# A recurrent-memory transformer layer on one core: rider queries' transposes, a store of extra rows and the tail's loads are moved in the queues

## The chip, the cores and the metric

The kernel runs on one core of one Trainium2 chip. The metric is the device time of one execution in microseconds (us). A core has five engines with an instruction stream each: TensorE (PE), VectorE (DVE), ScalarE (ACT), GpSimd (POOL) and SyncE (SP). Here SP and POOL mostly issue DMA transfers, which 16 DMA engines carry out.

## The reference

One layer on a sequence of 2048 tokens of width 640: attention with a recurrent memory, then a gated feed-forward network (FFN) of width 1728. Weights and inputs are bf16.

```python
mem = mem0                                   # 8 memory rows
for s in range(64):                          # segments of 32 tokens
    h = concatenate([mem, LN(x)[32*s : 32*s+32]])          # 40 rows
    q, k, v = h @ Wq, h @ Wk, h @ Wv         # 32 heads of 128
    p = softmax(mask(q @ k.T / sqrt(128)))   # memory rows see all; tokens: memory and earlier ones
    o = (p @ v) @ Wo
    mem = o[:8]; out[s] = o[8:]
h = x + out
y = h + ((relu(LN(h) @ Wg) * (LN(h) @ Wu)) @ Wd)
```

The memory of segment s + 1 is an output of segment s, so the 64 segments form a chain. Only the eight memory rows are in the chain: the projections of the tokens are not.

## The kernel before, in words

**Passes.** The loop over s makes one *pass* for each segment. TensorE projects 32 columns at a time: the 8 memory rows of segment s and 24 *riders*, rows of tokens that a later segment needs. As 24 riders a pass are fewer than the 32 tokens that a segment takes, a fourth kind of work, the *extra units*, projects 32 more tokens in three passes of four (`extra_units`: keys in phase s % 4 = 2, queries in phase 3, values in phase 0). In phase 1 the same place holds `woe_pass`, the output projection of the memory rows of four segments (the *extra rows*), summed by `woe_sum` in the tile `at` and stored by `woe_store`. `filler` puts these units between the steps of the softmax, so that TensorE has work while other engines run.

A pass has this order on TensorE: K projection into banks BQ; Q projection into P0 and P1; `pick_mem` (L450), which takes the memory rows' queries out of the token tiles; V projection; `scores` (L569); memory probabilities times V (L606) among the filler; their transposes (L621); the output projection `wo_pass` (L641, 128 short matmuls); `pv_x` (L679). The result of `wo_pass` makes the memory rows of the next pass (`to_act`).

**Transposes by DMA.** Projections come out with tokens on the partitions, and are wanted the other way round. ACT and DVE copy them to `tok` tiles (`to_tok`), tiles 0 and 1 for K, 2 and 3 for Q, and also 2 and 3 for the extra units. SP's queue then issues `dma_t`, a crossbar transpose by DMA (L360): K's into `KS`, the attention output's into `oT`, the rider queries' into `QS` (`trans_q`), and in phases 2 and 3 those of the extra units into a tile `Kr` or again into `QS`. From `QS`, `evac_q` copies the riders' queries into the ring `Qr` on ACT. The V riders go by POOL's DMAs (`v_riders`). In the kernel before, `trans_q` comes right behind the Q projection in program order, and `evac_q` behind `exp_x`.

**Order and waits.** `_Graph` records each operation with the names it reads and writes, and each engine runs its own in program order. `solve` sets a wait wherever an operation reads what another engine wrote, writes what it reads, or overwrites it. An operation put on an engine's queue holds back all that follow it there. The lists `late` and `late_q` hold operations that are recorded in the next pass, behind the transposes of K and of `oT`, and behind the Q copies. `align` puts spare weight loads into TensorE's stream so that marked places in `wo_pass` (`MARKS`) lie at fixed places of blocks of 256 instructions.

**Tail.** In the last passes the FFN weights are loaded over the projection weights. `load_gate_up` loads `xn2T`, `Wg`, `Wu` and `Wgu`; `gate_up(0, j)` are the first FFN products, mixed with the last segments' output projections and extra rows; `ln2_load` loads rows of x and attention for the second layer norm; `h_rows` and `Wd` are loaded for the down projection.

Of the kernel before, what the change touches and what calls it, by code (L numbers as in the profile page):

```python
# [206 lines left out]
def build_kernel(nc, A_x, A_mem0, A_Wq, A_Wk, A_Wv, A_Wo, A_seg_len, B_W_gate, B_W_up, B_W_down, out):  # L207
    _, S, D = A_x.shape
    M = A_mem0.shape[1]
    _, H, Dh = A_Wq.shape  # L210
    SEG = int(A_seg_len)
    F = B_W_gate.shape[1]
    assert (S, D, M, H, Dh, SEG, F) == (2048, 640, 8, 32, 128, 32, 1728)
    NSEG = S // SEG
    DC = D // 128
    HD = H * Dh
    FC = (F + 127) // 128
# [82 lines left out]
    def bank_bf(b):  # L300
        return ps[:, b * 512:(b + 1) * 512].bitcast(BF16)
# [14 lines left out]
    def B(n):  # L316
        return ("B", n)
# [38 lines left out]
    def dma(dst, src, r=(), w=(), eng="sp"):  # L356
        add(eng, lambda e: e.dma_start(dst, src), r=r, w=w, dma=True)  # L357
# [94 lines left out]
            return ins  # L452
        add("pe", f, r=[("tok", 2), ("tok", 3), ("ident",)], w=[B(bk)])

    def trans_q():
        dma_t(QS[:].rearrange("p h t -> p (h t)").rearrange("p (k r) -> p k r", r=128), tokp[1][:, :],
              [("tok", 2), ("tok", 3)], [("QS",)])

    def copy_op(eng, dst, src, r, w):
        if eng == "act":  # L460
# [21 lines left out]
    def evac_q(src, skey, t0, n, lo, eng):  # L482
        for q, o, m, lo in pieces(t0, n, lo):
            copy_op(eng, Qr[:, :, q, M + o:M + o + m], src[:, :, lo:lo + m], [skey], [("Qr", q)])
# [93 lines left out]
    def exp_mem():  # L578
        add("act", lambda a: a.activation(ap(om, 0, [[8, 2], [16, 8], [1, 8]]), s_view(0, M), ACTF.Exp,
                                          scale=SCALE), r=[B(P0), B(P1)], w=[("om",)])  # L580
        for i in range(2):
            add("dve", lambda v, i=i: v.tensor_tensor(ap(Pbd, 256 * i, [[32, 8], [16, 2], [1, 16]]),
                                                      ap(om, 0, [[16, 8], [0, 2], [1, 16]]),
                                                      ap(mbd, 32 * i, [[0, 8], [16, 2], [1, 16]]), ALU.min),
                r=[("om",), ("mbd",)], w=[("Pbd", i)])

    def exp_x():
        add("act", lambda a: a.activation(ap(Px, 0, [[32, 2], [64, 8], [1, 32]]), s_view(M, M + SEG),  # L588
# [28 lines left out]
    def trans_om(tile):  # L617
        for a, b in enumerate((T0, P3)):
            def f(pe, a=a, b=b):
                for c in range(0, 128, tile):  # L620
                    i = pe.matmul(bank_bf(b)[c:c + tile, 0:128], om[:, a, c:c + tile], ident[:, :], is_transpose=True)  # L621
                return i
            add("pe", f, r=[("om",), ("ident",)], w=[B(b)])
        for a, b in enumerate((T0, P3)):
            copy_op("dve", ap(oT, 8 * SEG * a, [[2 * SEG, 4], [16 * SEG, 2], [SEG, 2], [1, M]]),
                    bank_bf(b)[:, 0:128].rearrange("p (k g e q) -> p k g e q", k=4, g=2, e=2), [B(b)], [("oT", "mn"[a])])

    def head_of(n):

# [34 lines left out]
    def store_attn(src, skey, s):  # L664

        dma(bass.AP(attn_d, SEG * s * D, [[160, 4], [D, SEG], [1, 160]]), src[:].rearrange("p c j -> p (c j)"), r=[skey],
            w=[("attn", s)], eng="pool")
# [60 lines left out]
    def load_attn(dst, i, r, key):  # L728
        dma(dst[:, :], attn_d[128 * i:128 * i + 128, :, :].rearrange("t g f -> t (g f)"), r=attn_keys(i) + r, w=[key])

    def ln2_load(i):
        u = i % 4
        dma(xt2[u][:, :], x_ap[128 * i:128 * i + 128, :], r=[("Wdone", 1), ("Wu", DC - 1)], w=[("xt2", u)])
        load_attn(at2[u], i, [("Wdone", 1), ("Wu", DC - 1)], ("at2", u))

    def ln2_front(i):
        par, u = (i // 4) % 2, i % 4
# [94 lines left out]

    def load_gate_up(after):
        free = [("Wdone", 0)] + after
        dma(xn2T[0][:, :, :], xn2_d[:, :, :], r=[("xn2_d", u) for u in range(4)] + free,
            w=[("xn2", 0, u) for u in range(4)], eng="pool")
        for n, (t, src) in enumerate(((Wg, B_W_gate), (Wu, B_W_up))):
            for c in range(DC):
                dma(t[:, c, :], src[128 * c:128 * c + 128, 0:FM], r=free, w=[(("Wg", "Wu")[n], c)], eng="pool")
            dma(Wgu[:, :, n * FR:(n + 1) * FR], src.rearrange("(c p) f -> p c f", p=128)[:, :, FM:F],  # L840
                r=free, w=[("Wgu", n)], eng="pool")

    PARTS = tuple((c,) for c in range(DC))
    WPARTS = (range(0, 3), range(3, 6), range(6, 9), range(9, 13), range(13, 16))
# [38 lines left out]
        add("dve", lambda v: v.tensor_tensor(bass.AP(at, 0, [[D, 64], [1, 320]]), tmp, bank(bk)[0:64, 0:320], ALU.add),  # L883
            r=[B(bk), ("at",)], w=[("at",)])

    def woe_store(b):
        for dg in range(2):
            dma(bass.AP(attn_d, 128 * b * D + 320 * dg, [[SEG * D, 4], [D, M], [1, 320]]),
                bass.AP(at, 32 * dg * D, [[D, 32], [1, 320]]), r=[("at",)] + [("attn", 4 * b + j) for j in range(4)],
                w=[("attne", b, dg)], eng="pool")  # L890

    late, late_q = [], []
    for s in range(NSEG):
# [20 lines left out]
        if s > 0:  # L914
            a, ks, kn = pass_act(s)
            t0, nr = rider_tokens(s)
            project(a, ks, 1, (0, 1), BQ, (0, 1), spare=16)
            ks = ks + kn
            project(a, ks, 1, (0, 1), BQ, (2, 3, 4), spare=24)
            to_tok(BQ[0], 0, "act")  # L920
            to_tok(BQ[1], 1, "dve")
            if last:
                break
            dma_t(KS[:].rearrange("p h t -> p (h t)").rearrange("p (k r) -> p k r", r=128), tokp[0][:, :],
                  [("tok", 0), ("tok", 1)], [("KS",)])
            trans_ox()
            for f in late:
                f()
            late = []
            project(a, ks, 0, (0, 1), (P0, P1), spare=40)  # L930
            to_tok(P0, 2, "act")
            to_tok(P1, 3, "dve")
            for f in late_q:
                f()
            late_q = []
            if nr and s < NSEG - 2:
                trans_q()
            loads()
            project(a, ks, 2, (0, 1), (P2, P3), (0, 1), spare=16)
            if s == NSEG - 2:  # L940
                trans8(tok[2], ("tok", 2), tok[3], ("tok", 3), T0)
                copy_op("dve", Qr[:, :, q, 0:M], slots(T0, 0, M), [B(T0)], [("Qm", q)])
                evac_q(slots(T0, 0, SEG), B(T0), t0, nr, M, "act")
            else:
                pick_mem(T0)
                copy_op("dve", Qr[:, :, q, 0:M], bank(T0)[:, 0:256].rearrange("p (h t) -> p h t", t=M), [B(T0)], [("Qm", q)])
            if nr:
                evac_k(KS, ("KS",), t0, nr, M, "dve")
            project(a, ks, 2, (0, 1), (P2, P3), (2, 3, 4), spare=24)
            to_v(P3, Vp, 1, ("Vp", 3), "dve")  # L950
            to_v(P2, Vp, 0, ("Vp", 0), "act", 0, 2)
            scores(s)
            exp_mem()
            to_v(P2, Vp, 0, ("Vp", 1), "act", 2, 4)
            exp_x()
            if nr:
                v_riders(t0, nr)
                if s < NSEG - 2:
                    evac_q(QS, ("QS",), t0, nr, M, "act")
        units, evac, nfin = extra_units(s)  # L960
        woe = s % 4 == 1 and s >= 5

# [9 lines left out]
            copy_op("dve", oTn[:, :, :], oT[:, :, 0:M], [("oT", "m"), ("oT", "n")], [("oTn",)])  # L972
        elif s > 0:
            copy_oTe(s - 1)
        if s == NSEG - 2:
            load_gate_up([("oTe", (s - 1) % 4)])
        norm_om()
        filler(2)
        filler(3)
        trans_om(128 if s % 4 < 2 else 32)  # L980
        mask_x()
        n = n_rows(nb) if s % 4 == 2 and ln else 128 if e2b is not None else 0
        if n:
# [4 lines left out]
        if woe:  # L988
            copy_op("dve", oTe[:, :, 0:M], oTn[:, :, :], [("oTn",)], [("oTe", 0)])
            woe_sum(BQ[0])  # L990
            woe_store(s // 4 - 1)
        wo_pass(T1, MARKS[s % 4] if s > 0 else None)
        to_act(s + 1, B(T1), bank(T1)[:, 0:160])
        if s >= 1:
            wo_rows(T1, wtok[s % 2], ("wtok", s % 2), "act")
            store_attn(wtok[s % 2], ("wtok", s % 2), s - 1)
        pv_x(s, P0)
        if n:
            dma_t(chunks_of(at[:, :])[:, :, 0:n], xt[0:n, :], [("xt",)], [("at",)])
# [76 lines left out]
    def rows(bk, p, s):  # L1076
        wo_rows(bk, wtok[p], ("wtok", p), "act")
        store_attn(wtok[p], ("wtok", p), s)
# [14 lines left out]
    pv_x(s, P0)  # L1093
    copy_op("act", oTe[:, :, M * ((s - 1) % 4):M * ((s - 1) % 4) + M], QS[:, :, 0:M], [("QS",)], [("oTe", (s - 1) % 4)])
    norm_x(P0)
    wo_pass(BQ[1], None, QS, [[("QS",)]] * 2, (0,))
    trans_pe(oT, [("oT", "m"), ("oT", "n"), ("oT", "x")])
    wo_pass(BQ[1], None, QS, [[("QS",)]] * 2, (1,))
    rows(BQ[1], 0, s - 1)
    copy_oTe(s)  # L1100
    gate_up(0, 0)
    for i in range(4, 8):
        ln2_load(i)
    dma(h_rows[0][:, :, :], h_d[:, :].rearrange("(u p) d -> p u d", p=128), r=[("h_d", u) for u in range(4)] +
        [("Wdone", 1), ("Wu", DC - 1)], w=[("h", 0, u) for u in range(4)], eng="pool")
    dma(Wd[:, 0:FC - 1, :], B_W_down[0:FM, :].rearrange("(j p) d -> p j d", p=128),
        r=[("Wdone", 1)], w=[("Wd", 0)], eng="pool")
    dma(Wd[FR:128, FC - 1, :], B_W_down[FM:F, :], r=[("Wdone", 1)], w=[("Wd", 1)], eng="pool")
    wo_pass(P0)
    rows(P0, 1, s)  # L1110
    gate_up(0, 1)
    woe_pass(P3, range(16))
    woe_sum(P3)
    woe_store(NSEG // 4 - 1)
    gate_up(0, 2)
    gate_up(0, 3)
    for par in range(2):
# [83 lines left out]
```

## Time and profile before

| | value |
|---|---|
| time, median of 3 runs | 1107.48 us (1104.06 to 1113.91) |
| span of the profiled run | 1109.9 us |
| TensorE clock, mean | 0.992 of full speed |
| PE busy | 1054.9 us |
| DVE, ACT, POOL busy | 608.7, 365.7, 290.5 us |
| matmuls of the K, Q and V projections (L419, L397; act_r) | 4277 x 384 ns, 3603 x 379 ns, overlapping |
| SP's transposes into QS, KS, oT | 76, 62 and 62; 3.2, 3.2 and 2.8 us to landing |
| POOL's V rider copies | 376 |
| share of the 16 DMA engines' span: SP's queue, POOL's queue | 41.2%, 9.3% |

The page lists, per engine, how long it was busy, and per group of instructions what ended the idle time before them. "Idle before <- X" names the last semaphore that came; "issue" names a wait that no semaphore in the profile explains. A DMA's time runs from the start of its issue to its landing. PEld is the weight load that goes with each matmul.

### The profile page before, as it was taken

The numbers are of one execution on the slowest core, as the hardware profiler recorded it, in microseconds if no ns is written. First come the engines' busy times: TensorE is split into PE (matmuls) and PEld (weight loads), VectorE is DVE, ScalarE is ACT, GpSimd is POOL, SyncE is SP. The second block draws the span as 40 slices with busy tenths as digits, with TensorE's granted clock in tenths as the row PEclk, the third lists the DMA queues.
The fourth block names the chain that finished last, engine by engine and source line by source line (L and its number), as shares of the span: only waits on it lengthen the run. The fifth ranks groups of instructions, "written<-read, shape, count | busy, mean of one in ns | idle before, by whom it ended". The sixth has DMA issues, their size and how long they took to land.

```text
span 1109.9 us, 56106 instructions
## 1 busy us (share of the span) xinstructions
PE 1054.9 (95%) x28040; PEld 510.8 (46%) x23478; DVE 608.7 (55%) x1673; ACT 365.7 (33%) x794; POOL 290.5 (26%) x583
## 2 busy tenths in 40 slices
PE   4679999999999999999999999999999998999998
PEld 3344544444545454545454445444444454444443
DVE  3245656565556565666666666565656553553532
ACT  1214333433343433333334333334333332231211
POOL 1013333333333332323232323232324151000000
PEclk9979999999999999999999999999999999999999
DMA  9936464646463636465756665554545557132100
GB/s 362 377 84 111 88 109 89 105 90 107 81 110 80 115 79 110 83 123 100 119 103 116 104 114 107 93 92 97 94 92 96 93 159 240 39 80 75 27 18 25
DMA packets 287788, 121.65 MB, mean 110 GB/s; under 512 B 263968, under 2 KB 277184, under 8 KB 287552
## 3 DMA queue, kind: packets, MB, share of 16 engines
q1 hardware_dynamic: 267824, 93.92, 41.2%
q0 software_dynamic: 19312, 23.89, 9.3%
q8 instruction: 202, 3.31, 1.2%
q14 instruction: 34, 0.28, 0.1%
q10 hardware_dynamic: 416, 0.26, 0.1%
HBM read 36.79 MB, written 7.21 MB: 40 GB/s over the span
## 4 chain that ended last, share of the span: by engine, by line
PE 86%; DMA 8%; SPq 3%; issue 1%; POOL 1%; DVE 1%; ACT 1%; DVEq 0%; ACTq 0%
PE ps L419 24%; PE ps L397 23%; PE ps L641 13%; PE ps L1030 10%; PE ps L655 3%; PE ps L679 3%; PE ps L569 3%; PE ps L1062 3%; DMA Wo<-in_A_Wo_dram 3%; SPq L357 3%; PE ps L606 2%; DMA QS<-tok 2%; DMA KS<-tok 2%; PE ps L450 2%; PE ps L621 1%
## 5 line engine op out<-in xcount | busy, mean ns | idle before, releaser
L419 PE MATMUL ps<-W,act_r 128*32 128x512 bf16 x4277 | 399.1, 384 | 8.8 <-DMA W<-in_A_Wv_dram 2.5
L397 PE MATMUL ps<-W,act_r 128*32 128x512 bf16 x3603 | 356.9, 379 | 0.3
L357 POOL DMA_DIRECT2D Vr<-Vp x376 | 187.6, 506 | 449.7 <-ACT Px L588 396.9
L419 PEld LDWEIGHTS ps<-W,act_r 128*32 128x32 bf16 x4277 | 121.5, 97 | 262.2 <-issue 170.2
L461 ACT ACTIVATE tok<-ps 128x512 bf16<-128x512 f32 x191 | 110.3, 594 | 237.2 <-PE ps L397 204.7
L641 PE MATMUL ps<-Wo,oT 128*32 128x160 bf16 x8192 | 161.8, 236 | 14.6 <-DMA Wo<-in_A_Wo_dram 8.0
L641 PEld LDWEIGHTS ps<-Wo,oT 128*32 128x32 bf16 x8192 | 147.0, 98 | 36.6 <-issue 16.7
L463 DVE CAST tok<-ps 128x512 bf16<-128x512 f32 x131 | 90.5, 691 | 131.5 <-PE ps L397 109.9
L461 ACT ACTIVATE Qr<-QS 128x512 bf16<-128x512 bf16 (+3 forms) x107 | 70.1, 682 | 61.0 <-DMA QS<-tok 60.5
L419 PE MATMUL ps<-W,act_e 128*32 128x512 bf16 x900 | 89.6, 381 | 0.0
L397 PE MATMUL ps<-W,act_e 128*32 128x512 bf16 x900 | 89.1, 379 | 0.0
L552 DVE STREAM_TRANSPOSE TBf<-ps 128x64 f32<-128x64 f32 (+1 forms) x128 | 33.5, 262 | 93.9 <-PE ps L641 93.8
L694 DVE TENSOR_TENSOR ox<-ps,rx 128x512 bf16<-128x512 f32 x128 | 82.4, 685 | 2.2
L461 ACT ACTIVATE Vp<-ps 128x256 bf16<-128x256 f32 (+1 forms) x126 | 48.5, 385 | 104.7 <-PE ps L397 102.2
L357 POOL DMA_DIRECT2D attn_d<-wtok x64 | 46.6, 728 | 126.8 <-ACT wtok L461 126.6
L1045 DVE TENSOR_TENSOR hT<-g,ps 128x512 bf16<-128x512 bf16 (+1 forms) x56 | 38.5, 688 | 53.7 <-PE ps L1030 49.8
L1030 PE MATMUL ps<-xn2T,Wu 128*128 128x512 bf16 x260 | 64.6, 379 | 0.0
L1030 PE MATMUL ps<-xn2T,Wg 128*128 128x512 bf16 x246 | 61.6, 379 | 1.1 <-issue 0.3
L1043 ACT ACTIVATE g<-ps 128x512 bf16<-128x512 f32 (+1 forms) x56 | 32.4, 592 | 89.4 <-PE ps L1030 89.4
L397 PE MATMUL ps<-Wd,hT 128*128 128x320 bf16 x224 | 61.0, 299 | 0.0
L1062 PE MATMUL ps<-Wd,hT 128*128 128x320 bf16 x224 | 61.0, 299 | 0.0
L463 DVE CAST Vp<-ps 128x512 bf16<-128x512 f32 x64 | 44.2, 691 | 30.4 <-PE ps L397 24.5
(114 smaller groups left out, 1145.8 us busy)
## 6 DMA issues: line engine op xcount, KB each, us to landing
Vr<-Vp POOLq DMA_DIRECT2D x124, 48.8 KB, 2.3
W<-in_A_Wk_dram SPq DMA_DIRECT2D x2, 2560.0 KB, 13.2
W<-in_A_Wq_dram SPq DMA_DIRECT2D x2, 2560.0 KB, 29.3
W<-in_A_Wv_dram SPq DMA_DIRECT2D x2, 2560.0 KB, 28.1
Wo<-in_A_Wo_dram SPq DMA_DIRECT2D x2, 2560.0 KB, 28.5
xt<-in_A_x_dram SPq DMA_DIRECT2D x30, 160.0 KB, 3.6
Vr<-Vp POOLq DMA_DIRECT2D x128, 32.5 KB, 1.9
attn_d<-wtok POOLq DMA_DIRECT2D x64, 40.0 KB, 2.9
```

The source lines that it names most:

```text
L357: add(eng, lambda e: e.dma_start(dst, src), r=r, w=w, dma=True)
L397: return pe.add_instruction(mybir.InstMatmult(name=nc.get_next_instruction_name(), engine=mybir.EngineType.PE, ins=[pe.lower_ap(rhs), pe.l ...
L419: ins = pe.matmul(*a, start=(c == 0), stop=(c == DC - 1), skip_group_check=True)
L461: add("act", lambda a: a.activation(dst, src, ACTF.Copy), r=r, w=w)
L463: add("dve", lambda v: v.tensor_copy(dst, src), r=r, w=w)
L552: add("dve", lambda v, lo=lo, hi=hi: v.transpose(TBf[:, lo:hi, :].rearrange("p c t -> p (c t)"), src[:, 32 * lo:32 * hi]), r=[wkey], w=[(" ...
L569: i = pe.matmul(bank((P0, P1)[g % 2])[p:p + (M if a else 32), 40 * k:40 * k + 40], lh, Qr[:, h, q, :], start=True, stop=True, skip_group_c ...
L641: i = pe.matmul(bank(bk)[32 * gg:32 * gg + 32, 0:160], src[:, hb, :], w[:, gg], start=(hb == ORDER[0]), stop=(hb == ORDER[31]), skip_group ...
L694: add("dve", lambda v, kh=kh: v.tensor_tensor(ox[:, :, kh, :], src[:, :, kh, 0:128], ap(rx, kh, [[2, 4], [0, 128]]), ALU.mult), r=[B(b0 + ...
L1030: ins = pe.matmul(bank(bk), w[:, c, lo:lo + 128], xn2T[par][:, c, :], start=(c == 0), stop=(c == DC - 1))
L1045: add("dve", lambda v: v.tensor_tensor(hT[par][lo:128, j, :], g1[gi][lo:128, :], bank(bu)[lo:128, :], ALU.mult), r=[B(bu), ("g1", gi)], w= ...
L1062: i = pe.matmul(*a, start=(j == 0), stop=(j == FC - 1), skip_group_check=True)
```

## The change

It does four things to the order of work; nothing computed is changed.

1. `trans_q` of the riders moves from behind the Q projection to behind `v_riders`, and waits for a new name, `("qgo", 1)`, which the second operation on the memory probabilities (`Pbd`, L582) writes. The purpose is that this transpose runs after the probabilities of the memory rows, not beside the transposes of K and `oT`. Its `evac_q` on ACT moves behind `wo_rows` and `store_attn`.
2. `woe_store` is put into `late` with a read of `KS`: it goes when K's transpose in the next pass has landed.
3. `load_gate_up` is issued by SP instead of POOL, after the copies of `trans_om` (`("go", 1)`), and the small `Wgu` loads come last.
4. In the tail, `gate_up(0, 0)` comes before the last two segments' output projections; the loads of x, attention rows, `h_rows` and `Wd` wait for the last `woe_sum` (`("at",)`).

```diff
-    def trans_q():
+    def trans_q(after=()):
         dma_t(QS[:].rearrange("p h t -> p (h t)").rearrange("p (k r) -> p k r", r=128), tokp[1][:, :],
-              [("tok", 2), ("tok", 3)], [("QS",)])
+              [("tok", 2), ("tok", 3)] + list(after), [("QS",)])
...
-                r=[("om",), ("mbd",)], w=[("Pbd", i)])
+                r=[("om",), ("mbd",)], w=[("Pbd", i), ("qgo", i)])
...
-        dma(xt2[u][:, :], x_ap[128 * i:128 * i + 128, :], r=[("Wdone", 1), ("Wu", DC - 1)], w=[("xt2", u)])
-        load_attn(at2[u], i, [("Wdone", 1), ("Wu", DC - 1)], ("at2", u))
+        dma(xt2[u][:, :], x_ap[128 * i:128 * i + 128, :], r=[("Wdone", 1), ("at",)], w=[("xt2", u)])
+        load_attn(at2[u], i, [("Wdone", 1), ("at",)], ("at2", u))
...
-        dma(xn2T[0][:, :, :], xn2_d[:, :, :], r=[("xn2_d", u) for u in range(4)] + free,
-            w=[("xn2", 0, u) for u in range(4)], eng="pool")
-        for n, (t, src) in enumerate(((Wg, B_W_gate), (Wu, B_W_up))):
+        dma(xn2T[0][:, :, :], xn2_d[:, :, :], r=[("xn2_d", u) for u in range(4)] + free, w=[("xn2", 0, u) for u in range(4)])
+        both = (("Wg", Wg, B_W_gate), ("Wu", Wu, B_W_up))
+        for k, t, src in both:
             for c in range(DC):
-                dma(t[:, c, :], src[128 * c:128 * c + 128, 0:FM], r=free, w=[(("Wg", "Wu")[n], c)], eng="pool")
+                dma(t[:, c, :], src[128 * c:128 * c + 128, 0:FM], r=free, w=[(k, c)])
+        for n, (k, t, src) in enumerate(both):
             dma(Wgu[:, :, n * FR:(n + 1) * FR], src.rearrange("(c p) f -> p c f", p=128)[:, :, FM:F],
-                r=free, w=[("Wgu", n)], eng="pool")
+                r=free, w=[("Wgu", n)])
...
-    def woe_store(b):
+    def woe_store(b, after=()):
...
-            if nr and s < NSEG - 2:
-                trans_q()
             loads()
...
             if nr:
                 v_riders(t0, nr)
                 if s < NSEG - 2:
-                    evac_q(QS, ("QS",), t0, nr, M, "act")
+                    trans_q([("qgo", 1)])
...
-        if s == NSEG - 2:
-            load_gate_up([("oTe", (s - 1) % 4)])
         norm_om()
...
         trans_om(128 if s % 4 < 2 else 32)
+        if s == NSEG - 2:
+            load_gate_up([("oTe", (s - 1) % 4), ("go", 1)])
...
-            woe_store(s // 4 - 1)
+            late.append(lambda b=s // 4 - 1: woe_store(b, [("KS",)]))
...
             store_attn(wtok[s % 2], ("wtok", s % 2), s - 1)
+            if nr and s < NSEG - 2:
+                evac_q(QS, ("QS",), t0, nr, M, "act")
...
+    gate_up(0, 0)
     wo_pass(BQ[1], None, QS, [[("QS",)]] * 2, (0,))
     trans_pe(oT, [("oT", "m"), ("oT", "n"), ("oT", "x")])
     wo_pass(BQ[1], None, QS, [[("QS",)]] * 2, (1,))
     rows(BQ[1], 0, s - 1)
     copy_oTe(s)
-    gate_up(0, 0)
+    gate_up(0, 1)
+    wo_pass(P0)
+    rows(P0, 1, s)
+    woe_pass(P3, range(16))
+    woe_sum(P3)
+    woe_store(NSEG // 4 - 1)
     for i in range(4, 8):
         ln2_load(i)
     dma(h_rows[0][:, :, :], h_d[:, :].rearrange("(u p) d -> p u d", p=128), r=[("h_d", u) for u in range(4)] +
-        [("Wdone", 1), ("Wu", DC - 1)], w=[("h", 0, u) for u in range(4)], eng="pool")
+        [("Wdone", 1), ("at",)], w=[("h", 0, u) for u in range(4)], eng="pool")
     dma(Wd[:, 0:FC - 1, :], B_W_down[0:FM, :].rearrange("(j p) d -> p j d", p=128),
-        r=[("Wdone", 1)], w=[("Wd", 0)], eng="pool")
-    dma(Wd[FR:128, FC - 1, :], B_W_down[FM:F, :], r=[("Wdone", 1)], w=[("Wd", 1)], eng="pool")
-    wo_pass(P0)
-    rows(P0, 1, s)
-    gate_up(0, 1)
-    woe_pass(P3, range(16))
-    woe_sum(P3)
-    woe_store(NSEG // 4 - 1)
+        r=[("Wdone", 1), ("at",)], w=[("Wd", 0)], eng="pool")
+    dma(Wd[FR:128, FC - 1, :], B_W_down[FM:F, :], r=[("Wdone", 1), ("at",)], w=[("Wd", 1)], eng="pool")
```

More of the change, by code (lines that the diff above doesn't have):

```diff
@@ L625, in trans_om @@
             copy_op("dve", ap(oT, 8 * SEG * a, [[2 * SEG, 4], [16 * SEG, 2], [SEG, 2], [1, M]]),
-                    bank_bf(b)[:, 0:128].rearrange("p (k g e q) -> p k g e q", k=4, g=2, e=2), [B(b)], [("oT", "mn"[a])])
+                    bank_bf(b)[:, 0:128].rearrange("p (k g e q) -> p k g e q", k=4, g=2, e=2), [B(b)], [("oT", "mn"[a]), ("go", a)])
     def head_of(n):
@@ L884, in woe_sum @@
             r=[B(bk), ("at",)], w=[("at",)])
-    def woe_store(b):
+    def woe_store(b, after=()):
         for dg in range(2):
             dma(bass.AP(attn_d, 128 * b * D + 320 * dg, [[SEG * D, 4], [D, M], [1, 320]]),
-                bass.AP(at, 32 * dg * D, [[D, 32], [1, 320]]), r=[("at",)] + [("attn", 4 * b + j) for j in range(4)],
+                bass.AP(at, 32 * dg * D, [[D, 32], [1, 320]]), r=[("at",)] + [("attn", 4 * b + j) for j in range(4)] + list(after),
                 w=[("attne", b, dg)], eng="pool")
```

## The prediction

> **What bounds the kernel now.** I read the page first (busy shares, chain, queues), then the list of waits for PE, then PE's rows in order of time, cut into passes at L679 (the last block of a pass), and last the DMA packets beside the rows.
>
> ```profile
> span 1109.9 us, 56106 instructions
> PE 1054.9 (95%) x28040; PEld 510.8 (46%) x23478; DVE 608.7 (55%) x1673; ACT 365.7 (33%) x794; POOL 290.5 (26%) x583
> q8 instruction: 202, 3.31, 1.2%
> L461 ACT ACTIVATE Qr<-QS 128x512 bf16<-128x512 bf16 (+3 forms) x107 | 70.1, 682 | 61.0 <-DMA QS<-tok 60.5
> QS<-tok SPq DMA_TRANSPOSE x76, 3.2
> ```
>
> PE is busy 95% at a clock of 0.99: no other engine bounds the span, and only PE's holes can be won. The third line is PE's own instruction stream, fetched by DMA: 3.31 MB in 202 packets, 16.4 KB each. The last two say that ACT sits idle 60.5 us before copies out of QS, a transpose that takes 3.2 us from issue to landing.
>
> Between 92 and 895 us there are 60 whole passes, four phases (s % 4) of 15. Their means and minima are 13.53 and 13.23, 13.81 and 13.30, 13.60 and 13.20, 13.52 and 13.10 us, so 15 x (0.30 + 0.51 + 0.40 + 0.42) = 24.5 us lie above the best passes. By block, above the block's own minimum: output projection (L641, least 2.32 us) 10.5 us, of it 6.7 in phase 1; first projection (least 5.30) 6.1 us, of it 4.6 in phase 2; the projection before the scores 2.7; P.V (L679) 2.7. Pass 29, which began at 443.6, shows the cause, in the timeline:
>
> ```profile
> 450.20 1.27 SPq L360 DMA_TRANSPOSE QS<-tok  x1
> 451.73 0.49 DVE L582 TENSOR_TENSOR Pbd<-om,mbd 128x256 bf16<-128x256 bf16 x2 [0.29 <-ACT om L579]
> 452.56 3.95 POOL L357 DMA_DIRECT2D Vr<-Vp  x8 [7.43 <-ACT Px L588]
> 454.10 1.07 PE L641 MATMUL ps<-Wo,oT 128*32 128x160 bf16 x52
> 455.62 0.94 ACT L461 ACTIVATE Qr<-QS 128x256 bf16<-128x256 bf16 x2 [3.16 <-DMA QS<-tok]
> 455.84 1.50 PE L641 MATMUL ps<-Wo,oT 128*32 128x160 bf16 x76 [0.67 <-issue]
> 457.81 1.25 POOL L357 DMA_DIRECT2D attn_d<-at  x2 [1.30 <-DVE TBf L552]
> ```
>
> PE stops after 52 of 128 matmuls, with "issue" as the reason: nothing it waits for is late except its own instructions. The fetch packet for that place ran at 452.95 to 454.42, behind the QS transpose, whose packets filled all 16 DMA engines from 451.5 to 453.4. In passes that do not stop the same packet begins near 8.4 us after the pass's start; here at 9.3. The tail has the same hole:
>
> ```profile
> 919.25 0.94 PE L641 MATMUL ps<-Wo,QS 128*32 128x160 bf16 x43
> 922.55 0.58 PE L641 MATMUL ps<-Wo,QS 128*32 128x160 bf16 x21 [2.37 <-issue]
> 923.29 1.03 PE L1030 MATMUL ps<-xn2T,Wg 128*128 128x512 bf16 x4 [0.16 <-DMA Wu<-in_B_W_up_dram]
> ```
>
> Here 2.37 us go by while the FFN weights fill the DMA engines.
>
> **The Trainium skill.** "Runtime: NRT & Kernel Launch", section Instruction fetch mechanics: an engine's instructions come in blocks of 16 KiB, 256 instructions, over its own DMA queue, and crossing a block is mostly hidden. The trace agrees on the size; that it is hidden it contradicts where transposes are in the way (0.67 us above). "DMA: Bandwidth & Descriptors", section Queues, rings and completion order: each DMA engine takes packets from its queues in turn, so a fetch, a transpose and a GpSimd copy share it. The trace agrees: QS transposes that meet a fetch land in 4.6 to 5.5 us, the others in 3.1 to 3.2. "Advanced Engine Details and Errata", section Sequencer and Instruction Queues: a queued engine instruction waits for its semaphores before it goes; here ACT's copy above waited 3.16 us with the L882 copy of the extra rows behind it.
>
> **The change, part by part.**
>
> (1) *QS transpose later.* It now waits for the second L582 op, which ends 8.58 us into a pass, not 5.8 to 6.9. The second fetch (8.4 to 9.4) is then ahead of it. The transpose spends some 1.25 us on issue (its SPq row), so its packets lie at about 9.9 to 11.7, and the third fetch comes at 11.9 or later in undisturbed passes. I take 8 of the 10.5 us of the output projection as won, and 3.7 of the 4.6 us of phase 2, whose holes lie 20 matmuls into the pass, at a block's edge: they are the third fetch of phase 1, late because the second was. The rest stays for chance collisions. Sum -11.7.
>
> (2) *ACT's Qr copies after `wtok`.* The same 107 copies; they now run at 0.5 to 1.3 us of the next pass, ahead of that pass's first tok copy at 2.38 us, so they hide there. ACT no longer holds the extra units' copies (BQ) behind QS. Passes 36 and 47 lost 0.84 and 1.0 us in P.V's tail that way: -1.8.
>
> (3) *New wait.* The extra units of phases 2 and 3 write tok 2 and 3 on ACT, and now must wait for the QS transpose that reads them. Issue 8.60 + 3.2 = 11.8; two copies, 1.08 us, end at 12.9; PE needs the banks at 13.1 to 13.2, so landings up to 3.37 us are free. With the landings of KS (54 readable, median 3.2, three over 3.6) the overrun is 1.8 us over 30 passes; with those of today's QS (19 of 47 over 3.6) 15 us. KS has a fetch ahead of it, as QS will: I take 4.
>
> (4) *Second QS transpose of phase 3.* It overwrites QS, so it waits for the copies of (2): 0.47 + 0.84 = 1.31 us into phase 0, where it used to start before the pass began. Behind it: PE's pick of the memory rows (L450) needs tok 2 and 3, written at 4.54, and these wait for the landing. 1.31 + 3.05 (the least) = 4.36 costs nothing; with the 15 late landings of today (3.05 to 5.47) the mean overrun is 0.54, 8 us in all. A fetch begins at 2.05 or later in that phase, while the transpose is still being issued; such cases land in 3.5 to 3.9, 0.3 to 0.65 us too late: I take 0.4 x 15 = +6. Pass 48 shows the price: PE waited 0.5 us for a QS landing 4.97 us in.
>
> (5) *Extra rows' store after KS.* 15 x 2 DMAs, 0.61 us of POOL each, nothing behind them until the V copies at 8.9 us, so the move is free. In pass 18 two row stores lay under KS, which landed in 4.91 us, not 3.2, and PE lost 1.25 us: -1.2.
>
> (6) *Tail.* The weights' issue moves from POOL, where it starts at 906.7 after the V copies, to SP, at about 906; 4.9 MB at the 400 GB/s of the page's busiest slices end near 920.5, not 923.2. `gate_up(0, 0)` goes first, so PE waits from 917 to 920.5 for Wu, but then 11.8 us of work (Wo halves 1.3 + 1.2, transposes 0.55, two gate_up 2.05 each, Wo 2.3, extra rows 2.4) run with empty DMA engines to 932.3, where they ended at 932.9. The loads of `xt2`, `at2`, h and Wd wait for the extra rows (932): 4.1 MB, 10 us, the first rows due at 942, Wd at 958. Between -2.5 and +1: I take -1.
>
> Sum: -11.7 - 1.8 + 4 + 6 - 1.2 - 1 = -5.7, from a median of 1107.5; with two thirds of (4)'s price taken for the case that the fetch slips in behind, -8. I forecast 1100.
>
> **The rivals.** *Everything fits*: QS lands in 3.1 to 3.3 everywhere, (3) and (4) cost 1 us each, (1) brings 13. For it: KS, with a fetch in its issue, does so. 1107.5 - 13 - 1.8 + 2 - 1.2 - 2 = 1091.5. *A wait in place of the one removed, slower*: the QS packets now run beside the V copies of POOL (8.9 to 12.9) and the third fetch. The one transpose issued wholly beside them, in pass 59, landed in 5.47 us. For a landing of 4.3 the overrun in (3) is 0.95 x 30 = 28, (4) 10, less the 15.7 won in the loop and 1 in the tail: +21, 1129. Against it: in passes 40 and 44 POOL issued V copies while QS's packets ran; the copies' packets came after them, and QS landed in 3.1. *Gain given back in full*: (3) 8, (4) 8: 1107.
>
> The timeline of ACT at passes 47 and 48 shows both new waits as they look when they bite:
>
> ```profile
> 702.90 0.84 ACT L461 ACTIVATE Qr<-QS 128x768 bf16<-128x768 bf16 x1 [3.48 <-DMA QS<-tok]
> 703.65 1.06 ACT L461 ACTIVATE tok<-ps 128x512 bf16<-128x512 f32 x2
> 709.87 0.60 ACT L461 ACTIVATE tok<-ps 128x512 bf16<-128x512 f32 x1 [2.08 <-DMA QS<-tok]
> ```
>
> The first held the tok copies until pass 48 should have begun; the last is PE's 0.5 us.
>
> **How the numbers follow.** Forecast 0.45 (its spread, 1093 to 1106, is two thirds within 1%); everything fits 0.2; given back 0.13; slower 0.22. Faster by over 1% means below 1096.4: 0.2 + 0.17 = 0.37. Slower by over 1%, above 1118.6: 0.2. The rest, 0.43, is within. The range leaves out about 1 in 10 on each side: 1086 to 1126.
>
> **What would show it.** Right: output projections of 2.32 in phase 1; the second fetch before 8.6 us; no ACT wait on QS before L883; KS in phase 2 at 3.2. Wrong: ACT's tok copies of phases 2 and 3 idle on QS beyond 12 us of a pass, P.V's block over 1 us there, L450 late in phase 0, or a tail where the gate matmuls wait past 922.

## The result, and the profile after

The changed kernel takes 1185.24 us (median of 4 runs, 1179.2 to 1188.67), the kernel before 1109.97 (4 runs beside it): a ratio of 1.068, interval 1.061 to 1.075. The forecast was 1100, with a range to 1126.

The lines of the page after that answer to those shown of the kernel before, and from the list of DMA issues two, with the median from issue to landing at the end:

```profile
PE 1067.3 (90%) x28054; PEld 516.7 (44%) x23482; DVE 607.8 (51%) x1673; ACT 359.5 (30%) x794; POOL 282.9 (24%) x570
...
L461 ACT ACTIVATE tok<-ps 128x512 bf16<-128x512 f32 x191 | 110.6, 595 | 366.4 <-DMA QS<-tok 180.7
...
L461 ACT ACTIVATE Qr<-QS 128x512 bf16<-128x512 bf16 (+3 forms) x107 | 70.2, 688 | 7.1 <-DMA QS<-tok 7.0
```

```profile
QS<-tok SPq DMA_TRANSPOSE x76, 4.9
KS<-tok SPq DMA_TRANSPOSE x62, 3.2
```

The work is the same, but PE is busy 90% of the span, not 95%. ACT's idle time before the Qr copies (61.0 us before) has all but gone (7.1), and 180.7 us of idle time on the same transposes stand before the `tok` copies instead. QS lands in 4.9 us, not 3.2; KS, elsewhere in the pass, still in 3.2. That the wait moved costs nothing by itself, as ACT has time; what it costs PE is in the list of waits (total, times, longest):

```profile
ACT tok L461 <- DMA QS<-tok: 180.7, 41, 6.7
...
PE ps L419 <- ACT tok L461: 39.7, 18, 3.4
...
ACT tok L461 <- DMA Kr<-tok: 16.9, 8, 2.4
...
PE ps L419 <- issue: 15.1, 12, 2.9
...
PE ps L450 <- DVE tok L463: 9.2, 16, 1.5
```

PE waits for ACT's `tok` copies to free the banks BQ (second line), and for the tokens that `pick_mem` reads (last line). The second line is not all of it: holes at the same place stand under "issue" too (fourth line), and under DVE where its `ox` operation ended later than the copy (8.3 us). A sum by passes, cut as in the prediction, holds them all. Phases 0 to 3 now take 14.12, 13.53, 15.85 and 16.00 us a pass (13.53, 13.81, 13.60, 13.52 before): 15 x (0.59 - 0.28 + 2.25 + 2.48) = 75.6 us, which is all but about 1 us of the longer span. The rest of the span, from the end of pass 62, is 201.3 us, 200.9 before.

One pass of phase 2 in the timeline of the kernel after (it begins at 433.35; start, length, and in brackets the idle time before):

```profile
441.99 2.06 SPq L360 DMA_TRANSPOSE QS<-tok  x1
...
442.30 4.00 POOL L357 DMA_DIRECT2D Vr<-Vp  x8 [0.66 <-ACT Px L588]
...
443.62 2.40 PE L641 MATMUL ps<-Wo,oT 128*32 128x160 bf16 x128
...
448.07 1.09 ACT L461 ACTIVATE tok<-ps 128x512 bf16<-128x512 f32 x2 [5.88 <-DMA QS<-tok]
...
449.19 1.24 SPq L360 DMA_TRANSPOSE Kr<-tok  x1
...
449.31 0.62 PE L419 MATMUL ps<-W,act_r 128*32 128x512 bf16 x4 [2.71 <-ACT tok L461]
```

The output projection is whole (2.40 us, 128 matmuls without a hole), as the change wanted. But POOL issues its eight V copies from 442.3 to 446.3, right beside the transpose, which lands at 448.0, 6.0 us after its issue. ACT's two copies follow, and PE stands for 2.71 us at the start of the next pass. Kr, which waits for the same copies, goes at 449.2, 15.8 us after the pass's start; 12 before.

The hole costs PE more than its own length. From 449.23 to 452.64 us the clock granted to TensorE is halved. The matmuls of the last row above take 0.62 us, where the same four take 0.40 at full clock (as in the run with V copies behind QS, below). Two stretches of equal length, the slow one first (busy time of each engine, number of instructions, then PEclk, the granted clock):

```profile
core 0: us, PE busy (x) PEld busy (x) DVE busy (x) ACT busy (x) POOL busy (x), PEclk, DMA share, GB/s
449.23:452.64 3.41, 3.33 (x32) 0.86 (x20) 0.00 (x0) 0.95 (x3) 0.76 (x1) 0.50 0.81 89
452.64:456.05 3.41, 3.41 (x68) 0.79 (x28) 1.27 (x2) 1.18 (x2) 1.16 (x5) 1.00 0.65 106
```

There are 11 such stretches in the loop, each beside the end of a hole of 1.9 us or more at a pass's start; the loop of the kernel before has none. They fall on four first projections of phase 0 and seven of phase 3, which together last 17.5 us longer than their least time (6.0 and 11.5). So about 17 of the 75.6 us are work at half clock, not waiting. The executions agree: the lower the mean clock, the longer they took (1179.20 us at 0.987, 1183.99 at 0.981, 1186.48 at 0.976, 1188.67 at 0.975).

The tail, to hold against the rows shown before, and the granted clock in it:

```profile
997.85 1.68 PE L1031 MATMUL ps<-xn2T,Wu 128*128 128x512 bf16 x5 [0.47 <-DMA Wu<-in_B_W_up_dram]
999.46 1.29 PE L641 MATMUL ps<-Wo,QS 128*32 128x160 bf16 x64
```

```profile
995.36:998.77 3.41, 2.94 (x8) 0.85 (x7) 1.42 (x3) 0.60 (x1) 0.00 (x0) 0.50 0.34 73
```

The hole of 2.37 us within Wo's 64 matmuls (second row) is gone. In its place P.V of the last pass ends late, and the first gate products take 4.25 us, against 2.04: they run at half clock too.

### The profile page after: what moved, and what is told of

The parts are those of the page before. It is cut to its first block, busy times and chain, and to the rows that moved or that the text cites. A ratio compares the mean times of both kernels' runs of the same rounds, so it can differ in the third digit from the quotient of the medians.

```text
span 1186.9 us, 56105 instructions
## 1 busy us (share of the span) xinstructions
PE 1067.3 (90%) x28054; PEld 516.7 (44%) x23482; DVE 607.8 (51%) x1673; ACT 359.5 (30%) x794; POOL 282.9 (24%) x570
## 4 chain that ended last, share of the span: by engine, by line
PE 68%; DMA 22%; SPq 3%; issue 2%; ACT 2%; DVE 2%; DVEq 0%; ACTq 0%
PE ps L419 19%; PE ps L397 18%; DMA QS<-tok 15%; PE ps L1031 10%; PE ps L641 8%; DMA Kr<-tok 3%; PE ps L655 3%; SPq L357 3%; PE ps L569 3%; PE ps L1063 3%; DMA Wo<-in_A_Wo_dram 2%; PE ps L450 2%; PE ps L679 2%; ACT tok L461 1%; PE ps L606 1%
## 5 line engine op out<-in xcount | busy, mean ns | idle before, releaser
L419 PE MATMUL ps<-W,act_r 128*32 128x512 bf16 x4281 | 413.0, 392 | 70.4 <-ACT tok L461 39.7
L397 PE MATMUL ps<-W,act_r 128*32 128x512 bf16 x3599 | 370.7, 390 | 0.2 <-issue 0.2
L419 PEld LDWEIGHTS ps<-W,act_r 128*32 128x32 bf16 x4281 | 128.5, 99 | 333.3 <-issue 231.0
L461 ACT ACTIVATE tok<-ps 128x512 bf16<-128x512 f32 x191 | 110.6, 595 | 366.4 <-DMA QS<-tok 180.7
L641 PE MATMUL ps<-Wo,oT 128*32 128x160 bf16 x8192 | 159.2, 236 | 10.8 <-DMA Wo<-in_A_Wo_dram 8.9
L1031 PE MATMUL ps<-xn2T,Wg 128*128 128x512 bf16 x260 | 65.6, 383 | 0.4 <-ACT wtok L461 0.4
```

The costliest lines, as they stand in the source:

```text
L397: return pe.add_instruction(mybir.InstMatmult(name=nc.get_next_instruction_name(), engine=mybir.EngineType.PE, ins=[pe.lower_ap(rhs), pe.l ...
L419: ins = pe.matmul(*a, start=(c == 0), stop=(c == DC - 1), skip_group_check=True)
L461: add("act", lambda a: a.activation(dst, src, ACTF.Copy), r=r, w=w)
L641: i = pe.matmul(bank(bk)[32 * gg:32 * gg + 32, 0:160], src[:, hb, :], w[:, gg], start=(hb == ORDER[0]), stop=(hb == ORDER[31]), skip_group ...
L1031: ins = pe.matmul(bank(bk), w[:, c, lo:lo + 128], xn2T[par][:, c, :], start=(c == 0), stop=(c == DC - 1))
```

## The experiments

The theory, from these lines: step (3) is the right wait, but QS lands in about 5 us, because POOL's V copies share the DMA engines with it. Rivals: PE's own instruction fetch, or the late place as such, makes it land late; or the other edits cost something.

**Undo the transpose's move, keep the rest.** `trans_q()` and `evac_q` at their old places in the changed kernel.

> The changed kernel with parts (1) and (2) undone: the rider transpose and its Qr copies back at their old places, the store of the extra rows, the tail weights and the later loads as changed. Theory (all of the loss comes from the rider transpose that now lands about 2 us later than in step (3), in front of ACT's tok copies of phases 2 and 3): 1105 to 1110 us, passes of phases 2 and 3 back at 13.5 to 13.6 us. Rival (the other three edits cost something of their own, in the loop or the tail): 1118 us or more.

Measured: 1109.37 us, ratio to before 1.0003 (0.9988 to 1.0018). The store, the tail weights and the later loads together can't be told from nothing, to within 2 us.

**The transpose's move alone**, in the kernel before.

> The kernel before with parts (1) and (2) alone. Theory: 1180 to 1190 us, as the whole change, with phases 2 and 3 at 15.8 to 16.0 us a pass. Rival (the parts need each other, the store behind KS or the tail takes part in the loss): below 1165 us.

Measured: 1180.54 us, ratio 1.064 (1.062 to 1.066); phases 2 and 3 at 15.47 and 15.87 us, phase 2 a little under what was expected. So the move is the loss, to within 5 us.

**Another tile for phase 2's extra keys.**

```diff
-                    to_tok(BQ[i], 2 + i, e)
+                    to_tok(BQ[i], (0 if j == 1 else 2) + i, e)
...
-                dma_t(Kr[q][:].rearrange("p h t -> p (h t)").rearrange("p (k r) -> p k r", r=128), tokp[1][:, :],
-                      [("tok", 2), ("tok", 3)], [("Kr", q)])
+                dma_t(Kr[q][:].rearrange("p h t -> p (h t)").rearrange("p (k r) -> p k r", r=128), tokp[0][:, :],
+                      [("tok", 0), ("tok", 1)], [("Kr", q)])
```

> The changed kernel, but in phase 2 the extra units' keys are copied to tok 0 and 1, which K's transpose has freed by then, and are transposed from there; phase 3 stays as it is. QS still lands as late. Theory (the write-after-read wait on tok 2 and 3 is what stops PE): phase 2's hole before the end of P.V goes (2.25 us x 15 = 34) and, as Kr goes at 12 us again, most of the 0.7 us of phase 3's first projection (10): about 1143 us, phase 2 at 13.6 us, phase 3 still at 15 or more. Rival (the DMA engines are crowded and PE's own instructions come late, whichever tile is used): phase 2 stays at 15 us or more, 1175 us or more.

Measured: 1151.67 us. Phase 2 is back at 13.47 us with QS landing even later there (6.72 us median), and the end of P.V there lasts no more than 0.64 us in any pass: the hole is the wait on `tok` 2 and 3, not a crowd in front of PE's instructions. The 8 us missing from the expected 1143 are in phase 3 (16.36 us). Kr, beside the V copies too, lands 5.9 us after an issue at 11.6, 4 us into phase 3, and K's own `tok` copies there now wait for it. The expectation for that part was wrong. The loop of this kernel has no stretch at half clock, so that some of what it won is the clock's.

**V copies behind QS.**

```diff
-                dma(Vr[q][z:z + m, :, :], Vp[a:a + m, :, :], r=[("Vp", 0), ("Vp", 1), ("Vp", 3), ("Vp1",), ("Vr1", q)],
+                dma(Vr[q][z:z + m, :, :], Vp[a:a + m, :, :], r=[("Vp", 0), ("Vp", 1), ("Vp", 3), ("Vp1",), ("Vr1", q), ("QS",)],
...
-                v_riders(t0, nr)
                 if s < NSEG - 2:
                     trans_q([("qgo", 1)])
+                v_riders(t0, nr)
```

> The changed kernel, but POOL's V rider copies wait until QS has landed. Theory A (QS lands in 5.2 us instead of 3.2 because POOL's V copies share the DMA engines with it): QS lands in 3.2 to 3.5 us, ACT's wait on QS in phases 2 and 3 goes, 1095 to 1110 us. Theory B (the third fetch of PE's instructions, or the transpose's place in the pass, makes it slow): QS still lands in 4.5 us or more and the time stays above 1160 us. Both half: 1130 to 1150 us.

Measured: 1163.8 us. Theory A has its landing time, and not its total. The same pass as above in this kernel's timeline (it begins at 418.44):

```profile
427.07 1.27 SPq L360 DMA_TRANSPOSE QS<-tok  x1
...
428.70 2.40 PE L641 MATMUL ps<-Wo,oT 128*32 128x160 bf16 x128
...
430.31 1.09 ACT L461 ACTIVATE tok<-ps 128x512 bf16<-128x512 f32 x2 [3.04 <-DMA QS<-tok]
430.85 4.00 POOL L357 DMA_DIRECT2D Vr<-Vp  x8 [3.64 <-DMA QS<-tok]
...
431.43 1.23 SPq L360 DMA_TRANSPOSE Kr<-tok  x1
...
431.66 0.40 PE L419 MATMUL ps<-W,act_r 128*32 128x512 bf16 x4
```

QS lands 3.2 us after its issue (median of the late ones 3.07, against 5.15 in the changed kernel), and PE goes on without a hole: the ends of P.V in phases 2 and 3 lose 2 us in all, not 61. The time did not follow, because the V copies now run into the next pass: K's transpose in phase 3 lands in 5.66 us (3.2), and phase 0's first projection, behind the second QS transpose, takes 6.84 us (both medians). The cause of the late landing is shown; the cure only moved the collision.

**V copies left out from segment 8 on**, in the changed kernel and in the kernel before.

> The changed kernel with the V rider copies left out from segment 8 on (the V ring keeps old rows, which changes the output). Theory (V copies beside the transpose are the cause of its late landing): QS lands in 3.1 to 3.3 us, no hole at the end of P.V, no collision of V copies with KS as when they were put behind QS: 1093 to 1108 us. Rival (the third fetch of PE's instructions, or the late place as such, costs most): above 1140 us.

> The control of the other run without V rider copies: the kernel before with them left out from segment 8 on (output changed). Theory: the copies cost the kernel before little, 1100 to 1108 us; the difference between the two runs without V copies is then the sum of the prediction's steps without (3): -10 to +2 us. Rival: as with the copies, the changed kernel is 40 us or more slower than this one.

Measured: 1133.22 and 1104.48 us. V copies cost the changed kernel 1185.2 - 1133.2 = 52 us and the kernel before (1109.8 in these runs) 1109.8 - 1104.5 = 5: at least 47 of the 75 us go with them, with what follows from their collision with QS. But 29 us remain between the two kernels without them, where -10 to +2 was expected. Pass by pass, 12 us of this lie before segment 8, where both still have V copies (three passes there take 16.5 to 17.0 us, much as in the changed kernel). From segment 8 on the changed kernel loses 67 us with V copies and 19 without, 16 of these in phase 0. So a second cause is there, and the list of waits of the changed kernel without V copies says where to look:

```profile
PE ps L450 <- DVE tok L463: 19.1, 15, 1.8
...
PE ps L419 <- ACT tok L461: 4.9, 2, 2.9
```

The 15 passes of phase 0 wait at `pick_mem`: that is step (4). The two holes of the second line lie before segment 8.

**Only the Qr copies late.** `trans_q()` in the changed kernel without its wait, so near its old time.

> The changed kernel, but the rider transpose does not wait for the memory probabilities: it goes as soon as tok 2 and 3 are written, as in the kernel before, and only its Qr copies stay late. This leaves part (2) and the wait of part (4) alone. Theory (the loss is from the late landing; the copies' move is free, and the second transpose of phase 3 waits for them until 1.3 us into phase 0, then lands in 3.1 us without V copies beside it): 1105 to 1113 us, first projection of phase 0 5.3 to 5.5 us, no hole at the end of P.V in phases 2 and 3. Rival (the place of the copies costs by itself): 1125 us or more.

Measured: 1130.65 us, ratio 1.018 (1.015 to 1.021): the rival's number, but from one phase alone. Phase 0's first projection takes 6.92 us (median; 5.30 before), phases 1 to 3 are those of the kernel before (13.61, 13.42, 13.48). Waits of this kernel:

```profile
DVE tok L463 <- DMA QS<-tok: 37.1, 15, 3.4
...
PE ps L450 <- DVE tok L463: 20.2, 15, 1.8
```

The second QS transpose goes at 1.23 us into phase 0, close to the 1.31 of step (4), but lands 4.7 us later.

**Phase 3's copies back to the old place**, all else as in the run just told.

> The run with only the copies late (1130 us), but in phase 3 the copies go back to their old place, so that the second QS transpose does not wait for them. Theory (the whole loss of that run is step (4)): 1104 to 1111 us, phase 0 at 13.4 to 13.6 us. Rival (late copies cost in the other phases as well): 1118 us or more.

Measured: 1113.75 us, ratio 1.004 (1.002 to 1.006); phase 0 at 13.51. Step (4) is 1130.65 - 1113.75 = 17 of that run's 21 us. The expected top of 1111 was missed by 3; where those lie isn't settled.

**What delays the second QS transpose.** In phase 3 the store of the attention rows waits for the next KS.

> The run with only the copies late (1130 us), but in phase 3 POOL's store of the attention rows waits until K's transpose of the next pass has landed, so that its 64 packets are not beside the second QS transpose. Theory F (PE's instruction fetch, 2 to 4 us into phase 0, catches that transpose before it is complete): it still lands in 4.3 to 5.1 us, phase 0 stays at 14.5 us or more, 1124 to 1132 us. Theory S (the store's packets slow it): it lands in 3.0 to 3.6 us, phase 0 near 13.7 us, 1108 to 1115 us.

Measured: 1129.47 us, in the range of theory F. A pass of phase 0 (begun at 376.86) in this kernel, first from the chain of waits (start, length, what), then its DMA packets from 378 to 383 (packets, MB, share of the 16 engines):

```profile
378.08 4.81 DMA QS<-tok
...
382.98 0.70 DVE tok L463
...
383.73 0.36 PE ps L450 x8
```

```profile
q1 hardware_dynamic: 1990, 0.50, 83.1%
q8 instruction: 1, 0.02, 1.1%
```

There is no POOL packet on the engines, only transposes and one fetch of PE's instructions. The fetch runs from 380.4 to 381.3, when QS's last packets have just begun and K's transpose is next; QS is done at 382.9. Of the 14 cases in this trace whose landing can be read 13 landed in 4.3 to 4.9 us, each with a fetch that began 1.2 to 2.9 us after the issue; the other, with a fetch at 2.68, landed in 3.34. So the store is cleared, and the fetch is in every slow case. That the fetch is the cause isn't shown: it is in the quick case too, K's transpose stands behind in all of them, and no run took the fetch or K's transpose away. When it begins does matter: in the changed kernel without V copies the same transpose landed in 3.84 to 4.76 us in the five passes whose fetch began within 0.9 us of the issue, and in 4.75 to 5.16 us in the six where it began 2.6 us or more behind.

**Late only where nothing waits.** The kernel before, with `trans_q` and its copies late in phases 0 and 1 alone, and the store behind KS; then the same with V copies behind QS in these phases.

> The kernel before with the rider transpose and its copies late in phases 0 and 1 alone, where no extra units write tok 2 and 3 behind it, and with the extra rows' store behind KS; phases 2 and 3 and the tail as before. Theory: QS still lands in about 5 us in phases 0 and 1, but nothing on PE's path waits for it before the next pass; phases 0 and 1 fall to 13.4 us a pass (from 13.5 and 13.8), so 15 x (0.1 + 0.4) = 7 us are won: 1098 to 1104 us. Rival (a late QS spoils the next pass too, by its copies or its packets): 1108 us or more.

> As the run with the late transpose in phases 0 and 1 alone, and in these two phases POOL's V copies wait until QS has landed. Theory (V copies beside the transpose and the fetch behind it gave the single long passes of phase 1 there): QS lands in 3.1 us, no pass of phase 1 above 14.4 us, phases 0 and 1 at 13.3 and 13.4 us a pass, V copies running on into phases 1 and 2 cost less than 0.1 us a pass: 1098 to 1104 us. Rival (V copies that run into the next pass meet K's transpose there, as they did in phase 3 when all phases had them late): 1110 us or more.

Measured: 1108.81 us, ratio 0.998 (0.997 to 1.000), the rival's range, and 1108.49 us, ratio 0.999 (0.997 to 1.001), between theory and rival. In the first, phase 0 fell to 13.33 us and phase 1 to a median of 13.30, but two passes of phase 1 took 16.2 us, with PE waiting on its own instructions. In the second, phase 0 fell to 13.29, one such pass remained (15.65), and phase 2, into which the V copies now run, rose to 13.91 (13.60 before). Neither beats the kernel before by what a run can tell.

**The tail alone**, in the kernel before.

> The kernel before with part (6) alone: tail weights by SyncE's queue, first gate products earlier, the other loads later; the loop is untouched. Theory from the run without the transpose's move (1.0003 for parts (5) and (6) together, with 2 us less in phase 2): the tail costs 1 to 3 us more than before, 1110 to 1113 us, ratio 1.001 to 1.003. Rival (step (6) as forecast, -1 us, and the store's move worth nothing): 1107 to 1109 us, ratio 0.998 to 1.000.

Measured: 1110.08 us, ratio 1.0003 (0.998 to 1.002): between the two, and not to be told from nothing.

## Why the prediction was wrong, by its steps

(1) *Right in mechanism, its second half did not come.* With the move alone phase 1's output projections lose 0.2 us in all above the 2.32 us (6.6 before); in the changed kernel the gain over all phases is 7.5 us (8 forecast). The 3.7 us of phase 2's first projection were not won: 7.4 us are lost there, 4.6 before. They are not the QS transpose's: with V copies behind QS, where it lands in 3.07 us, 4.1 us are still lost, and without V copies 1.6 with the move and 1.9 in the kernel before. So most of this loss goes with the V copies, wherever QS stands; the step took QS for the cause.

(2) *Right.* ACT's wait before the Qr copies fell from 60.5 to 7.0 us. The 1.8 us forecast can't be told apart, and the 4 us left open above may belong here.

(3) *The term that failed: the landing time.* The chain was the one named (transpose, `tok` copies, BQ banks, PE), but the step read the landing from KS, which has a fetch ahead of it and no V copies. Of 54 late QS transposes in the trace of the changed kernel none lands within the 3.37 us that were free: 3.58 to 6.73, median 5.15. For +4 the loss is 59.6 us at the ends of P.V in phases 2 and 3 (60.7 us above 0.63, less 1.1 before). Two more costs are in no step. One is the clock: the 17.5 us lost at half clock stand behind these holes. The other is Kr: it goes 4 us later, lands inside phase 3 and holds copies there, and the eight passes of phase 3 at full clock lose 4.4 us in the first projection, 3.6 more than all 15 did before. (With 2.8 in phase 2's first projection and 6.4 in phase 0's at full clock, less 7.5 at the output projections and 6.6 at shorter blocks elsewhere, this is the loop's 75.6, to within 0.2.) The prediction had both pieces of evidence and weighed them wrongly: passes 40 and 44, where V copies were issued while QS ran, showed copies whose packets came after QS's; pass 59, the one with V copies beside it from the start, landed in 5.47 us.

(4) *Right wait; its size came out in the changed kernel, in part by luck.* There the 11 passes of phase 0 at full clock lose 7.1 us in the first projection, 6.4 more than all 15 did before, and 6 was forecast; in the other four the slow projection hides the wait. But the issue came at 0.85 us, not 1.31, and the landing in 3.94 us (medians). Where the issue came at 1.23 us, close to what was worked out, with only the copies late, the landing took 4.7 us, not 3.5 to 3.9, and the step cost 17 us, nearly three times the forecast.

(5) and (6) *Nothing.* -1.2 and -1 were forecast; together they measure 1.0003. In the tail the hole in the Wo products was filled, and the time came back in front of it: the first gate products, now earlier, take 2.2 us longer, 0.47 of it for `Wu`, and most of the rest at half clock. That the new order brings this slow stretch isn't shown: the run with late copies in phases 0 and 1 alone, which has the old tail, has a slow stretch there as well (granted clock 0.51 from 917.5 to 924.4 us). The weights' rate was read too high: the busiest slice of the page shows 377 GB/s, not 400.

The rival "a wait in place of the one removed" was the case. Its 1129 used a landing of 4.3 us; with 5.15 its overrun is nearly 1.8 us for 30 passes, 53 us instead of 28. (Its sum takes the tail's 1 us twice, as the 15.7 hold it already: 1130.) Its chance of 0.22 was too low, since every late QS runs beside V copies by its place: in the pass shown the two are released at 441.99 and 442.30, at the same step of the softmax.

One reading of the prediction does not hold as it stands: that QS transposes which meet a fetch land in 4.6 to 5.5 us, and the others in 3.1 to 3.2. In the kernel before, from segment 8 on, 21 of the 24 early QS transposes that landed within 3.25 us also had a fetch begin between issue and landing. V copies do not part the slow from the quick there either: without them 15 of 42 took 4.4 us or more. What makes an early QS slow stays open. (The 60 passes begin at 78.7 us, not at 92.)

## What to carry to other kernels

When an edit moves a transfer, read its new landing time from a transfer that has the same neighbours on the DMA engines at that time, above all another engine's queue, not from one of the same size. Ask of each transfer what else is released at the same step: two that start together collide in every pass, not now and then. A buffer with three users (here `tok` 2 and 3: queries, extra units, the transposes that read them) turns a late read into a stalled writer, and the writer is two steps from the engine that stops. And count the granted clock when a hole has been made: here work behind the holes ran at half speed, which a sum of waits alone does not show.

## What the runs showed of the hardware

A transpose has 1056 packets, and they go in two bursts of 528. Where other packets hold it up, new ones trickle until 528 have begun, and only then does the rate come back: in 27 of 49 late QS transposes of the changed kernel the last 48 of the first burst took over 0.25 us, and in one of them the first 48 of the second. DMA packets from the transpose's issue to its landing in the two passes of phase 2 shown above, first the changed kernel (441.9 to 448 us), then V copies behind QS (427 to 430.8):

```profile
q1 hardware_dynamic: 1056, 0.26, 44.1%
q0 software_dynamic: 310, 0.23, 21.7%
```

```profile
q1 hardware_dynamic: 1056, 0.26, 35.4%
q0 software_dynamic: 96, 0.04, 5.9%
```

The transposes' packets (q1) are the same; POOL's (q0) are 310 against 96. With POOL's V copies out of the way the first burst is out 1.88 us after issue, the last packet begins at 2.59 and the landing comes at 3.07 (medians of 52). Beside V copies these are 2.40, 3.76 and 5.15 (54): each burst is stretched, and the landing comes 1.4 us after the last packet has begun, not 0.5. "DMA: Bandwidth & Descriptors" of the Trainium skill, section Queues, rings and completion order, has the engines take packets of their queues in turn; the trace agrees, and adds that a transpose pays for it at each of its bursts. It works both ways: the V copies themselves land in 3.9 us beside the transpose, 2.3 and 1.9 before (the two larger sizes).

The stretches at half clock are 3.41 us long, and matmuls go half as fast in them (32 against 68 above). In the loop of the changed kernel each of the 11 began between 0.6 us before and 0.7 us after the end of a hole of 1.93 to 3.40 us; of 15 holes over 1.9 us these 11 had one. With the move alone there were 8, beside holes of 2.06 to 3.13 us. In the run with another tile three holes over 1.9 us had none. Why some holes have one and others not isn't shown, and no run was made to test it.
